# Banks, half tiles, placed turns and split casts in a fused linear-attention and gated-FFN kernel

## The chip, the core and the metric

The kernel runs on one core of one Trainium2 chip. A core has TensorE (PE, matrix products, which write to PSUM), VectorE (DVE), ScalarE (ACT), GpSimd (POOL) and SyncE (SP, here a queue that issues DMAs). Each engine works through its own queue in order and waits for the others by semaphores. PSUM is used here as one tile `ps` of 8 banks with 512 float32 columns each.

The metric is the device time of one execution in microseconds, as the median of several runs. The profile comes from one further execution and has its own time.

## The reference

Linear attention with a cosine weight, and behind it a feed-forward network with a GELU gate. B = 8 batches, H = 8 heads, S = 576 positions, D = 64; 4608 tokens, 512 channels, 1536 hidden columns:

```python
def phi(x, c, s):                       # c, s: cos and sin of pi/2 * pos/S
    r = np.maximum(x, 0.0)
    return np.concatenate([r * c, r * s], axis=-1)
q_p = phi(q, cos_w, sin_w)
k_p = phi(k, cos_w, sin_w)
kv = np.einsum('bhsf,bhsd->bhfd', k_p, v)
z = np.sum(k_p, axis=2)
num = np.einsum('bhsf,bhfd->bhsd', q_p, kv)
den = np.einsum('bhsf,bhf->bhs', q_p, z)[..., None] + 1e-06
attn = num / den
...
g = x @ w_gate                          # x: attn as [4608, 512]
gelu = 0.5 * g * (1.0 + erf(g * inv_sqrt2))
val = x @ w_val
out = gelu * val @ w_out
```

## The kernel before

**Tiles.** A batch of 576 positions is held as tiles j = 0 to 4. Tiles 0 to 3 have 128 rows; tile 4 has 64 positions, which stand in every other row of its 128, the rows between being zero. Tokens are split into blocks of the FFN: block 0 has 576 tokens (batch 0), the blocks after it 512 each, the last 448.

**Attention of a batch.** `scale` makes `qp` and `kp` (relu times cos, relu times sin) on DVE ("v") or ACT ("s"), `cast_v` the bfloat16 copy `vx` of v (line 138), four heads to an instruction. `kv_half(b, g)` makes kv and z of four heads with 20 matmuls (line 151), and `kv_evac` copies them out. `qp` is turned to `qT`: in batches 0 and 1 by PE (`q_by_pe`, line 311) and a copy out of PSUM (`q_evac`, line 317), later by a DMA (`turn_q`). `numer_mm(b, t, bank, g)` multiplies four heads of query tile t with kv (line 167); the two calls of a tile fill two banks. `norm` (lines 179 to 182) divides by the last column on DVE and writes `xb`; `numer` is both. `xb` is turned to channels by tokens, `xT`: in batches 0 and 1 by PE and a copy (`x_by_pe`, lines 325 to 329), later by a DMA (`turn_x`). Of tile 4 the copy takes every other column.

**FFN.** `gv_unit(n, jt, c0, w, gb, vb)` makes 128 hidden columns of w tokens: four matmuls g into bank gb (line 213), GELU on ACT (line 218), four matmuls v into bank vb (line 222), and the product to `hT` on DVE (line 226). `o_tile` multiplies 128 tokens of `hT` by the output weights in twelve matmuls (line 245), which `o_half` splits in two; `o_store` copies the sum on ACT (line 275) and issues the store.

**Order.** It is written out by hand: each engine runs its instructions in the order of the text. Batch 0 has nothing to run beside it, so its units of jt 0 to 3 are cut into pieces of tokens, and between them stand the numerators, turns and copies of the query tiles 1 to 4 (lines 371 to 414). `dummies` are matmuls of zeros that fill PE's time. Numerators of batch 0 all go to banks 6 and 7. POOL issues the weights in four steps: two of them before, two after x0 is written (lines 385 to 387), then the output weights, and when their first half has landed, SP loads q, k and v of batch 1 (lines 417 to 423). Then jt 4 to 11 run in pairs of 256 and 320 tokens. Lines 429 to 486 hold the last units of block 0, its output tiles with batch 1's attention between them, and batch 1's first units. From there on `run_block(n)` runs a block's 12 units, and the table `after` places the work of the next batch behind them: for n = 1 to 6 batch n + 1 is scaled, cast (line 516) and run through `attn_step`; each block also holds the output tiles of the one before.

Of the kernel before, what the change touches and what calls it, by code (L numbers as in the profile page):

```python
# [12 lines left out]
ALU = mybir.AluOpType  # L13
# [3 lines left out]
def kernel(  # L17
# [35 lines left out]
    ps = pp.tile([128, 8, 512], FP32, name="ps")  # L53
# [5 lines left out]
    xT = sb.tile([128, CT, N_TOK], BF16, name="xT")  # L59
# [5 lines left out]
    qT = [sb.tile([128, NJ + 1, H, 128], BF16, name=f"qT{i}") for i in range(2)]  # L65
# [4 lines left out]
    ident = sb.tile([128, 128], BF16, name="ident")  # L70
# [89 lines left out]
    def kv_evac(b, g, bank, eng):  # L160
        src = ps[:, bank, 0:4 * (D + 1)].rearrange("p (h e) -> p h e", e=D + 1)
        dst = kv[b % 2][:, 4 * g:4 * g + 4, 0:D + 1]
        (nc.scalar.copy if eng == "s" else nc.vector.tensor_copy)(dst, src)

    def numer_mm(b, t, bank, g):
        for h in range(4 * g, 4 * g + 4):
            nc.tensor.matmul(  # L167
                ps[:, bank + g, (h % 4) * (D + 1):(h % 4 + 1) * (D + 1)],
                lhsT=qT[b % 2][:, t, h, :],
                rhs=kv[b % 2][:, h, 0:D + 1],  # L170
                start=True, stop=True,
            )

    def norm(xb, bank, g0, g1):

        n = g1 - g0
        nd = ps[:, bank + g0:bank + g1, 0:4 * (D + 1)].rearrange("p g (h e) -> p g h e", e=D + 1)
        den = rot.tile([128, 2, 4], FP32, name="den")
        nc.vector.tensor_scalar(den[:, 0:n], nd[:, :, :, D], EPS, None, op0=ALU.add)
        rec = rot.tile([128, 2, 4], FP32, name="rec")  # L180
        nc.vector.reciprocal(rec[:, 0:n], den[:, 0:n])
        nc.vector.tensor_tensor(  # L182
            xb[:, g0:g1], nd[:, :, :, 0:D],
            rec[:, 0:n, :, None].to_broadcast([128, n, 4, D]), op=ALU.mult,
        )

    def new_xb():
        return rot.tile([128, 2, 4, D], BF16, name="xb", bufs=4)

    def numer(b, t, bank):  # L190

        numer_mm(b, t, bank, 0)
        numer_mm(b, t, bank, 1)
        xb = new_xb()
        norm(xb, bank, 0, 2)
        return xb

    def turn_x(b, t, xb):
# [10 lines left out]
    def gv_unit(n, jt, c0, w, gb, vb, mid=()):  # L209

        p0 = starts[n] + c0
        for ct in range(CT):
            nc.tensor.matmul(  # L213
                ps[:, gb, 0:w], lhsT=wg_sb[:, ct, jt * 128:(jt + 1) * 128],
                rhs=xT[:, ct, p0:p0 + w], start=(ct == 0), stop=(ct == CT - 1),
            )
        gel = rot.tile([128, 512], FP32, name="gel", bufs=3)
        nc.scalar.activation(gel[:, 0:w], ps[:, gb, 0:w], AF.Gelu)  # L218
        for f in mid:
            f()  # L220
        for ct in range(CT):
            nc.tensor.matmul(  # L222
                ps[:, vb, 0:w], lhsT=wv_sb[:, ct, jt * 128:(jt + 1) * 128],
                rhs=xT[:, ct, p0:p0 + w], start=(ct == 0), stop=(ct == CT - 1),
            )
        nc.vector.tensor_mul(hT[n % 2][:, jt, 64 + c0:64 + c0 + w], gel[:, 0:w], ps[:, vb, 0:w])  # L226
# [12 lines left out]
            return rows[p0 // 2:(p0 + n) // 2, j:j + 6:5]  # L239
        return rows[:, NJ]  # L240

    def o_half(n, m, bank, half):
        c0 = 128 * m - starts[n] + 64
        for jt in range(6 * half, 6 * half + 6):
            nc.tensor.matmul(  # L245
                ps[:, bank, :], lhsT=hT[n % 2][:, jt, c0:c0 + 128], rhs=wo_sb[:, jt, :],
                start=(jt == 0), stop=(jt == JT - 1),
            )
        if half == 1:
            o_store(m, bank)  # L250

    def o_tile(n, m, bank):

        o_half(n, m, bank, 0)
        o_half(n, m, bank, 1)

    def o_last(m, bank):

# [36 lines left out]
    def load_q(b):  # L295
        load(qf, q, b)
# [10 lines left out]
    def q_by_pe(b, j, bank, eng, h0=0, h1=H):  # L307

        qb = ps[:, bank, :].bitcast(BF16).rearrange("p (h t) -> p h t", h=H)
        for h in range(h0, h1):  # L310
            nc.tensor.transpose(out=qb[:, h, :], in_=qp[:, j, h, :], identity=ident)  # L311
        if eng is not None:
            q_evac(b, j, bank, eng, h0, h1)

    def q_evac(b, j, bank, eng, h0=0, h1=H):
        qb = ps[:, bank, :].bitcast(BF16).rearrange("p (h t) -> p h t", h=H)
        (nc.vector.tensor_copy if eng == "v" else nc.scalar.copy)(qT[b % 2][:, j, h0:h1], qb[:, h0:h1])  # L317

    def x_by_pe(b, t, xb, bank, eng, c0=0, c1=CT):
        p0 = b * S + t * 128  # L320
        cp = nc.vector.tensor_copy if eng == "v" else nc.scalar.copy
        xb2 = xb.rearrange("p g h d -> p (g h d)")
        view = ps[:, bank, 0:256].bitcast(BF16).rearrange("p (c t) -> p c t", c=CT)
        for ct in range(c0, c1):
            nc.tensor.transpose(out=view[:, ct], in_=xb2[:, ct * 128:(ct + 1) * 128], identity=ident)  # L325
        if t < NJ:
            cp(xT[:, c0:c1, p0:p0 + 128], view[:, c0:c1])  # L327
        else:
            cp(xT[:, c0:c1, p0:p0 + 64], view[:, c0:c1, 0:128:2])
# [8 lines left out]
    a4, b4 = (0, 4), (4, 8)  # L338
# [27 lines left out]
    q_evac(0, 0, 0, "v", *b4)  # L366
    q_evac(0, 1, 1, "v", *b4)
    kv_evac(0, 0, 4, "s")
    dummies(1, 7)
    kv_half(0, 1, 5, "s")  # L370
    x0 = new_xb()
    numer_mm(0, 0, 6, 0)
    norm(x0, 6, 0, 1)
    dummies(1, 4)
    numer_mm(0, 0, 6, 1)
    norm(x0, 6, 1, 2)
    q_evac(0, 2, 2, "s", *a4)
    dummies(1, 5)
    x_by_pe(0, 0, x0, 4, "s", 0, 2)
    dummies(2, 5)  # L380
    x_by_pe(0, 0, x0, 4, "s", 2, 4)
    x1 = numer(0, 1, 6)
    q_evac(0, 2, 2, "s", *b4)

    nc.gpsimd.tensor_copy(tiny[0:1, 1:2], x0[0:1, 1, 3, D - 1:D])
    load_w(4, 8)
# [1 line left out]


    A, Bw = (0, 256), (256, 320)  # L390
    gv_unit(0, 0, 0, 128, 0, 1)
    gv_unit(0, 1, 0, 128, 5, 4)
    x_by_pe(0, 1, x1, 0, "s")
    q_evac(0, 3, 3, "s", *a4)
    x2 = numer(0, 2, 6)
    gv_unit(0, 0, 128, 128, 5, 1)
    gv_unit(0, 1, 128, 128, 0, 4)
    q_evac(0, 3, 3, "s", *b4)
    x_by_pe(0, 2, x2, 2, "v")
    x3 = numer(0, 3, 6)  # L400
    gv_unit(0, 2, *A, 5, 1)
    q_by_pe(0, 4, 3, "s")
    gv_unit(0, 3, *A, 0, 4)
    x_by_pe(0, 3, x3, 2, "s")
    x4 = numer(0, 4, 6)
    gv_unit(0, 0, 256, 128, 5, 1)
    gv_unit(0, 1, 256, 128, 0, 4)
    gv_unit(0, 0, 384, 128, 5, 1)
    gv_unit(0, 1, 384, 128, 0, 4)
    x_by_pe(0, 4, x4, 3, "v")  # L410
    gv_unit(0, 2, *Bw, 5, 1)
# [84 lines left out]
    def L(f, *a):  # L496
        return lambda: f(*a)
# [78 lines left out]
```

## Time and profile before

| | |
|---|---|
| median of 3 runs | 334.9 us (334.8 to 335.13) |
| the profiled execution | 334.5 us, its span 332.4 us |
| TensorE clock granted, mean | 0.997 |
| four matmuls of 128, 256, 320, 512 columns, start to start | 0.22, 0.44, 0.54, 0.86 us |
| DVE product of 128x512 / of 128x128 | 0.69 / 0.29 us |
| GELU of 128x512 / of 128x128 on ACT | 0.60 / 0.28 us |
| cast of four heads of v (128x1280) on DVE / on ACT | 0.95 / 1.25 us |
| copy of 128x512 bfloat16 out of PSUM on DVE / on ACT | 0.41 / 0.59 us |

The span runs from the first to the last instruction; the time of the execution has 2.1 us around it. A row of the order of time has start, duration, engine, line, operation, output, inputs, shape and count, and in brackets the idle time of the engine before it and who ended it. Rows of several matmuls run into one another, since a matmul's duration includes its way through the array; where PE is free is read from the distance of starts.

### The profile page before, as it was taken

How to read it: one execution, taken by the hardware profiler on the slowest of the kernel's cores; microseconds unless marked ns; L12 is line 12 of the kernel's file. 1: busy time of each engine (PE TensorE's matmuls, PEld its weight loads, DVE VectorE, ACT ScalarE, POOL GpSimd, SP SyncE). 2: the span in 40 equal slices, each digit the busy share in tenths (PEclk: the TensorE clock that was granted, in tenths of full speed). 3: DMA queues.
4: the chain of work that ended last, by engine and by line, in shares of the span. 5: the costliest groups of instructions: out<-in, count | busy, mean ns of one | idle time of the engine just before them, and what ended most of it. 6: DMA issues, size and time to landing. Idle time of an engine off the chain costs nothing.

```text
span 332.4 us, 6000 instructions
## 1 busy us (share of the span) xinstructions
PE 322.4 (97%) x2281; PEld 171.3 (52%) x2281; DVE 177.2 (53%) x397; ACT 150.3 (45%) x278; POOL 19.7 (6%) x39
## 2 busy tenths in 40 slices
PE   7888999999999999999999999999999999999995
PEld 2576866755445444544455445444455444444443
DVE  5965478876674548454755576457635323222210
ACT  6764469683473237423742275226532322322321
POOL 2350010000100001000100010001000100000000
PEclk9999999999999999999999999999999999999998
DMA  7999988999379945996499449983723021000024
GB/s 237 257 186 207 240 299 268 318 219 351 66 123 247 345 80 100 263 333 95 86 263 321 110 77 210 374 132 59 180 48 77 20 65 32 32 34 32 34 65 95
DMA packets 84381, 54.66 MB, mean 164 GB/s; under 512 B 49408, under 2 KB 79872, under 8 KB 84352
## 3 DMA queue, kind: packets, MB, share of 16 engines
q1 hardware_dynamic: 78128, 49.10, 58.1%
q0 software_dynamic: 5792, 4.72, 9.4%
q10 hardware_dynamic: 432, 0.46, 0.4%
q8 instruction: 18, 0.29, 0.4%
q14 instruction: 11, 0.09, 0.1%
HBM read 37.75 MB, written 9.44 MB: 142 GB/s over the span
## 4 chain that ended last, share of the span: by engine, by line
PE 89%; DVE 5%; ACT 2%; issue 1%; DMA 1%; DVEq 0%; ACTq 0%
PE ps L245 27%; PE ps L213 26%; PE ps L222 26%; PE ps L167 3%; PE ps L124 3%; DVE vx L138 3%; PE ps L151 2%; PE ps L311 1%; PE ps L264 1%; ACT kp L134 1%; DMA out_dram<-o_sb 1%; DVE hT L226 1%; PE ps L325 1%; ACT gel L218 0%; DVE xb L182 0%
## 5 line engine op out<-in xcount | busy, mean ns | idle before, releaser
L226 DVE TENSOR_TENSOR hT<-gel,ps 128x512 bf16<-128x512 f32 (+5 forms) x130 | 77.0, 596 | 131.3 <-PE ps L222 128.1
L213 PE MATMUL ps<-xT,wg_sb 128*128 128x512 bf16 (+5 forms) x520 | 114.7, 343 | 1.4 <-ACT xT L327 0.7
L222 PE MATMUL ps<-xT,wv_sb 128*128 128x512 bf16 (+5 forms) x520 | 114.6, 343 | 0.8 <-DVE hT L226 0.8
L218 ACT ACTIVATE gel<-ps 128x512 f32<-128x512 f32 (+5 forms) x130 | 68.2, 525 | 84.7 <-PE ps L213 83.4
L245 PE MATMUL ps<-wo_sb,hT 128*128 128x512 bf16 x420 | 96.2, 379 | 0.0
L222 PEld LDWEIGHTS <-wv_sb 128*128 128x128 bf16 x520 | 49.1, 98 | 46.2 <-issue 1.0
L213 PEld LDWEIGHTS <-wg_sb 128*128 128x128 bf16 x520 | 47.0, 98 | 41.1 <-issue 1.5
L245 PEld LDWEIGHTS <-hT 128*128 128x128 bf16 x420 | 40.2, 98 | 45.9
L275 ACT COPY o_sb<-ps 128x512 f32<-128x512 f32 x35 | 20.5, 585 | 75.9 <-PE ps L245 72.8
L182 DVE TENSOR_TENSOR xb<-ps,rec 128x512 bf16<-128x512 f32 (+1 forms) x41 | 27.8, 679 | 1.5
L134 ACT ACTIVATE kp<-kf,sin_c 128x512 bf16<-128x512 f32 (+1 forms) x41 | 25.3, 679 | 0.5 <-DMA kf<-in_k_dram 0.5
L132 DVE TENSOR_SCALAR qp<-qf,cos_c 128x512 bf16<-128x512 f32 (+1 forms) x45 | 21.3, 516 | 0.7 <-DMA qf<-in_q_dram 0.7
L167 PEld LDWEIGHTS <-qT 128*128 128x128 bf16 x320 | 15.2, 98 | 9.2 <-issue 2.0
L134 ACT ACTIVATE qp<-qf,sin_c 128x512 bf16<-128x512 f32 (+1 forms) x31 | 19.2, 664 | 0.2 <-DMA qf<-in_q_dram 0.2
L132 DVE TENSOR_SCALAR kp<-kf,cos_c 128x512 bf16<-128x512 f32 (+1 forms) x45 | 18.0, 451 | 1.1 <-DMA kf<-in_k_dram 1.1
L167 PE MATMUL ps<-kv,qT 128*128 128x65 bf16 x320 | 17.0, 193 | 0.6 <-ACT qT L317 0.3
L206 POOL COPY xT<-xr 128x256 bf16<-128x256 bf16 x6 | 2.4, 400 | 205.3 <-DMA xr<-xb 205.3
L124 PE MATMUL ps<-junk 128*128 128x512 bf16 x37 | 11.4, 451 | 1.7 <-DVE par_i L101 1.7
L151 PEld LDWEIGHTS <-kp 128*128 128x128 bf16 x320 | 11.1, 97 | 3.5 <-issue 2.5
L151 PE MATMUL ps<-vx,kp 128*128 128x65 bf16 x320 | 11.9, 193 | 0.5
L138 DVE CAST vx<-vf 128x1280 bf16<-128x1280 f32 (+1 forms) x13 | 11.7, 934 | 0.3 <-DMA vf<-in_v_dram 0.3
L231 POOL COPY hT<-hT 128x768 bf16<-128x768 bf16 x8 | 7.6, 946 | 40.1 <-DVE hT L226 40.1
(54 smaller groups left out, 91.8 us busy)
## 6 DMA issues: line engine op xcount, KB each, us to landing
out_dram<-o_sb SPq DMA_DIRECT2D x38, 128.0 KB, 2.4
qf<-in_q_dram SPq DMA_DIRECT2D x7, 640.0 KB, 6.1
kf<-in_k_dram SPq DMA_DIRECT2D x7, 640.0 KB, 7.6
out_dram<-o_sb SPq DMA_DIRECT2D x16, 256.0 KB, 3.5
vf<-in_v_dram SPq DMA_DIRECT2D x6, 640.0 KB, 9.1
qf<-in_q_dram SPq DMA_DIRECT2D x7, 512.0 KB, 4.7
kf<-in_k_dram SPq DMA_DIRECT2D x7, 512.0 KB, 6.5
vf<-in_v_dram SPq DMA_DIRECT2D x6, 512.0 KB, 8.3
```

The source lines that it names most:

```text
L124: nc.tensor.matmul(ps[:, bank, :], lhsT=junk[:, 0:128], rhs=junk, start=True, stop=True)
L132: nc.vector.tensor_scalar(d, s, col, 0.0, op0=ALU.mult, op1=ALU.max)
L134: nc.scalar.activation(d, s, AF.Relu, scale=col)
L138: cp(vx[b % 2][:, :, h0:h1, 0:D], vf[:, h0:h1].rearrange("p h j d -> p j h d"))
L151: nc.tensor.matmul(ps[:, bank, (h % 4) * (D + 1):(h % 4 + 1) * (D + 1)], lhsT=kp[:, j, h, :], rhs=vx[b % 2][:, j, h, 0:D + 1], start=(j == ...
L167: nc.tensor.matmul(ps[:, bank + g, (h % 4) * (D + 1):(h % 4 + 1) * (D + 1)], lhsT=qT[b % 2][:, t, h, :], rhs=kv[b % 2][:, h, 0:D + 1], sta ...
L182: nc.vector.tensor_tensor(xb[:, g0:g1], nd[:, :, :, 0:D], rec[:, 0:n, :, None].to_broadcast([128, n, 4, D]), op=ALU.mult,)
L213: nc.tensor.matmul(ps[:, gb, 0:w], lhsT=wg_sb[:, ct, jt * 128:(jt + 1) * 128], rhs=xT[:, ct, p0:p0 + w], start=(ct == 0), stop=(ct == CT - 1),
L218: nc.scalar.activation(gel[:, 0:w], ps[:, gb, 0:w], AF.Gelu)
L222: nc.tensor.matmul(ps[:, vb, 0:w], lhsT=wv_sb[:, ct, jt * 128:(jt + 1) * 128], rhs=xT[:, ct, p0:p0 + w], start=(ct == 0), stop=(ct == CT - 1),
L226: nc.vector.tensor_mul(hT[n % 2][:, jt, 64 + c0:64 + c0 + w], gel[:, 0:w], ps[:, vb, 0:w])
L245: nc.tensor.matmul(ps[:, bank, :], lhsT=hT[n % 2][:, jt, c0:c0 + 128], rhs=wo_sb[:, jt, :], start=(jt == 0), stop=(jt == JT - 1),)
```

## The change

Four things change.

1. Batch 0: the numerators of tiles 1 to 4 get banks 0 and 1, those of tile 1 right behind those of tile 0; the q copies of tile 2 move ahead on ACT; one filler matmul goes. The turns (`X`) and the numerators (`Y`) of the tiles stand in other places among the pieces of units, some of them between g and v of a unit (the argument `mid`). The pieces use banks 4 to 7 (the last two 0 to 3).
2. The last query tile of batches 0 and 1: `q_evac` copies only its 64 used columns, so numerators, norm and turn run on 64 rows, and the copy to `xT` is without a step.
3. `o_half` becomes `o_part` with any range of hidden tiles; the fourth output tile of block 0 runs in four parts instead of two, the first of them between the two halves of the numerators of batch 1.
4. In every block from n = 2 to 6 the second half of v is cast by ACT; before, DVE cast both halves there.

```diff
-    def numer_mm(b, t, bank, g):
+    def numer_mm(b, t, bank, g, rows=128):
         for h in range(4 * g, 4 * g + 4):
             nc.tensor.matmul(
-                ps[:, bank + g, (h % 4) * (D + 1):(h % 4 + 1) * (D + 1)],
-                lhsT=qT[b % 2][:, t, h, :],
+                ps[0:rows, bank + g, (h % 4) * (D + 1):(h % 4 + 1) * (D + 1)],
+                lhsT=qT[b % 2][:, t, h, 0:rows],
                 rhs=kv[b % 2][:, h, 0:D + 1],
                 start=True, stop=True,
             )
...
-    def o_half(n, m, bank, half):
+    def o_part(n, m, bank, j0, j1):
         c0 = 128 * m - starts[n] + 64
-        for jt in range(6 * half, 6 * half + 6):
+        for jt in range(j0, j1):
...
-        if half == 1:
+        if j1 == JT:
             o_store(m, bank)
...
-        (nc.vector.tensor_copy if eng == "v" else nc.scalar.copy)(qT[b % 2][:, j, h0:h1], qb[:, h0:h1])
+        cp = nc.vector.tensor_copy if eng == "v" else nc.scalar.copy
+        if j < NJ:
+            cp(qT[b % 2][:, j, h0:h1], qb[:, h0:h1])
+        else:
+            cp(qT[b % 2][:, j, h0:h1, 0:64], qb[:, h0:h1, 0:128:2])
...
+        rows = 128 if t < NJ else 64
         view = ps[:, bank, 0:256].bitcast(BF16).rearrange("p (c t) -> p c t", c=CT)
         for ct in range(c0, c1):
-            nc.tensor.transpose(out=view[:, ct], in_=xb2[:, ct * 128:(ct + 1) * 128], identity=ident)
-        if t < NJ:
-            cp(xT[:, c0:c1, p0:p0 + 128], view[:, c0:c1])
-        else:
-            cp(xT[:, c0:c1, p0:p0 + 64], view[:, c0:c1, 0:128:2])
+            nc.tensor.transpose(
+                out=view[:, ct, 0:rows], in_=xb2[0:rows, ct * 128:(ct + 1) * 128], identity=ident[0:rows, 0:rows],
+            )
+        cp(xT[:, c0:c1, p0:p0 + rows], view[:, c0:c1, 0:rows])
...
     kv_evac(0, 0, 4, "s")
+    q_evac(0, 2, 2, "s", *a4)
     dummies(1, 7)
     kv_half(0, 1, 5, "s")
-    x0 = new_xb()
+    q_evac(0, 2, 2, "s", *b4)
+    x0, x1 = new_xb(), new_xb()
     numer_mm(0, 0, 6, 0)
     norm(x0, 6, 0, 1)
     dummies(1, 4)
     numer_mm(0, 0, 6, 1)
     norm(x0, 6, 1, 2)
-    q_evac(0, 2, 2, "s", *a4)
-    dummies(1, 5)
+    numer_mm(0, 1, 0, 0)
+    numer_mm(0, 1, 0, 1)
+    norm(x1, 0, 0, 2)
     x_by_pe(0, 0, x0, 4, "s", 0, 2)
     dummies(2, 5)
     x_by_pe(0, 0, x0, 4, "s", 2, 4)
-    x1 = numer(0, 1, 6)
-    q_evac(0, 2, 2, "s", *b4)
...
-    gv_unit(0, 0, 0, 128, 0, 1)
-    gv_unit(0, 1, 0, 128, 5, 4)
-    x_by_pe(0, 1, x1, 0, "s")
+    xs = {1: x1}
+
+    def X(t, bank, eng):
+        return lambda: x_by_pe(0, t, xs[t], bank, eng)
+
+    def Y(t):
+        def f():
+            xs[t] = numer(0, t, 0, 128 if t < NJ else 64)
+        return f
+
+    gv_unit(0, 0, 0, 128, 5, 6)
+    gv_unit(0, 1, 0, 128, 4, 7, (X(1, 2, "s"), Y(2)))
     q_evac(0, 3, 3, "s", *a4)
-    x2 = numer(0, 2, 6)
-    gv_unit(0, 0, 128, 128, 5, 1)
-    gv_unit(0, 1, 128, 128, 0, 4)
+    gv_unit(0, 0, 128, 128, 5, 6)
+    q_by_pe(0, 4, 2, None)
+    gv_unit(0, 1, 128, 128, 4, 7)
+    X(2, 5, "v")()
     q_evac(0, 3, 3, "s", *b4)
-    x_by_pe(0, 2, x2, 2, "v")
-    x3 = numer(0, 3, 6)
-    gv_unit(0, 2, *A, 5, 1)
-    q_by_pe(0, 4, 3, "s")
-    gv_unit(0, 3, *A, 0, 4)
-    x_by_pe(0, 3, x3, 2, "s")
-    x4 = numer(0, 4, 6)
-    gv_unit(0, 0, 256, 128, 5, 1)
-    gv_unit(0, 1, 256, 128, 0, 4)
-    gv_unit(0, 0, 384, 128, 5, 1)
-    gv_unit(0, 1, 384, 128, 0, 4)
-    x_by_pe(0, 4, x4, 3, "v")
-    gv_unit(0, 2, *Bw, 5, 1)
-    gv_unit(0, 3, *Bw, 0, 4)
-    gv_unit(0, 0, 512, 64, 5, 1)
-    gv_unit(0, 1, 512, 64, 0, 4)
+    q_evac(0, 4, 2, "s")
+    gv_unit(0, 2, *A, 4, 6, (Y(3),))
+    gv_unit(0, 3, *A, 5, 7)
+    X(3, 3, "s")()
+    Y(4)()
+    gv_unit(0, 0, 256, 128, 4, 6)
+    gv_unit(0, 1, 256, 128, 5, 7)
+    gv_unit(0, 0, 384, 128, 4, 6, (X(4, 2, "v"),))
+    gv_unit(0, 1, 384, 128, 5, 7)
+    gv_unit(0, 2, *Bw, 4, 6)
+    gv_unit(0, 3, *Bw, 5, 7)
+    gv_unit(0, 0, 512, 64, 0, 3)
+    gv_unit(0, 1, 512, 64, 1, 2)
...
     numer_mm(1, 1, 2, 0)
+    o_part(0, 3, 5, 0, 2)
     numer_mm(1, 0, 0, 1)
...
-    o_half(0, 3, 5, 0)
+    o_part(0, 3, 5, 2, 6)
     y2 = numer(1, 2, 6)
     x_by_pe(1, 0, y0, 0, "s")
-    o_half(0, 3, 5, 1)
+    o_part(0, 3, 5, 6, 9)
     x_by_pe(1, 1, y1, 1, "s")
+    o_part(0, 3, 5, 9, 12)
...
-    y4 = numer(1, 4, 2)
+    y4 = numer(1, 4, 2, 64)
...
-        put(4 + s, L(cast_v, b, 0, 4), L(cast_v, b, 4, 8, "s" if n == 1 else "v"))
+        put(4 + s, L(cast_v, b, 0, 4), L(cast_v, b, 4, 8, "s"))
```

`norm`, `numer` and the rest of `x_by_pe` get the same argument `rows` and work on `0:rows` of their tiles.

More of the change, by code (lines that the diff above doesn't have):

```diff
@@ L172, in numer_mm, with norm @@
             )
-    def norm(xb, bank, g0, g1):
+    def norm(xb, bank, g0, g1, rows=128):
         n = g1 - g0
-        nd = ps[:, bank + g0:bank + g1, 0:4 * (D + 1)].rearrange("p g (h e) -> p g h e", e=D + 1)
+        nd = ps[0:rows, bank + g0:bank + g1, 0:4 * (D + 1)].rearrange("p g (h e) -> p g h e", e=D + 1)
         den = rot.tile([128, 2, 4], FP32, name="den")
-        nc.vector.tensor_scalar(den[:, 0:n], nd[:, :, :, D], EPS, None, op0=ALU.add)
+        nc.vector.tensor_scalar(den[0:rows, 0:n], nd[:, :, :, D], EPS, None, op0=ALU.add)
         rec = rot.tile([128, 2, 4], FP32, name="rec")
-        nc.vector.reciprocal(rec[:, 0:n], den[:, 0:n])
+        nc.vector.reciprocal(rec[0:rows, 0:n], den[0:rows, 0:n])
         nc.vector.tensor_tensor(
-            xb[:, g0:g1], nd[:, :, :, 0:D],
-            rec[:, 0:n, :, None].to_broadcast([128, n, 4, D]), op=ALU.mult,
+            xb[0:rows, g0:g1], nd[:, :, :, 0:D],
+            rec[0:rows, 0:n, :, None].to_broadcast([rows, n, 4, D]), op=ALU.mult,
         )
@@ L188, in new_xb, with numer @@
         return rot.tile([128, 2, 4, D], BF16, name="xb", bufs=4)
-    def numer(b, t, bank):
-        numer_mm(b, t, bank, 0)
-        numer_mm(b, t, bank, 1)
+    def numer(b, t, bank, rows=128):
+        numer_mm(b, t, bank, 0, rows)
+        numer_mm(b, t, bank, 1, rows)
         xb = new_xb()
-        norm(xb, bank, 0, 2)
+        norm(xb, bank, 0, 2, rows)
         return xb
@@ L248, in o_half @@
             )
-        if half == 1:
+        if j1 == JT:
             o_store(m, bank)
     def o_tile(n, m, bank):
-        o_half(n, m, bank, 0)
-        o_half(n, m, bank, 1)
+        o_part(n, m, bank, 0, JT)
     def o_last(m, bank):
```

## The prediction

> **What bounds the kernel now.** I read the first page, then the list of waits of TensorE (PE), then PE's order of time in three stretches, then the same stretches on VectorE (DVE) and ScalarE (ACT), and last the DMA landings. The page:
>
> ```profile
> span 332.4 us, 6000 instructions
> PE 322.4 (97%) x2281; PEld 171.3 (52%) x2281; DVE 177.2 (53%) x397; ACT 150.3 (45%) x278; POOL 19.7 (6%) x39
> PE 89%; DVE 5%; ACT 2%; issue 1%; DMA 1%; DVEq 0%; ACTq 0%
> ```
>
> PE is busy for 322.4 of 332.4 us and 89% of the chain that ended last runs on it. So time can only come from the stalls of PE and from PE work that goes away. The busy time of a matmul includes its drain, so short stalls hide in it: I count a stall by the distance of starts. Four in a row of 128 columns start 0.22 us after each other (18.41 to 18.63), of 256 columns 0.435, of 320 columns 0.545, of 64 columns 0.12, eight numerator matmuls take 0.26 (60.54 to 60.80).
>
> PE in order of time, first batch (columns: start, duration, engine and line, what, count, idle before and who ended it):
>
> ```profile
> 20.16 0.38 PE L213 MATMUL ps<-xT,wg_sb 128*128 128x128 bf16 x4 [0.42 <-ACT xT L327]
> 21.84 0.30 PE L167 MATMUL ps<-kv,qT 128*128 128x65 bf16 x4 [0.27 <-ACT qT L317]
> 26.61 0.38 PE L222 MATMUL ps<-xT,wv_sb 128*128 128x128 bf16 x4 [0.49 <-DVE hT L226]
> 28.24 0.72 PE L213 MATMUL ps<-xT,wg_sb 128*128 128x320 bf16 x4 [0.58 <-DVE xT L329]
> 31.23 0.28 PE L222 MATMUL ps<-xT,wv_sb 128*128 128x64 bf16 x4 [0.30 <-DVE hT L226]
> 31.35 0.60 PE L213 MATMUL ps<-xT,wg_sb 128*128 128x256 bf16 x4
> ```
>
> Each wait names one step of the chain numerators, norm, turn, copy to xT, next unit. From 17.71 (first g of the FFN) to 31.35 (`gv_unit(0, 4)`) are 13.64 us. The work in it: sixteen 128-column groups of four 3.57, four of 256 1.74, four of 320 2.18, four of 64 0.48, four turns 0.89, three numerators 0.78, eight q transposes 0.445: 10.09 us. **3.55 us is stall**, and from 31.35 on PE runs gapless to 58.4.
>
> The v casts: first PE in a block where ACT casts half of v (n = 1) and one where DVE casts both (n = 2), then DVE before the latter.
>
> ```profile
> 73.30 1.37 PE L151 MATMUL ps<-vx,kp 128*128 128x65 bf16 x40
> 103.69 1.62 PE L151 MATMUL ps<-vx,kp 128*128 128x65 bf16 x40
> ```
>
> ```profile
> 102.69 1.81 DVE L138 CAST vx<-vf 128x1280 bf16<-128x1280 f32 x2
> 104.42 0.67 DVE L226 TENSOR_TENSOR hT<-gel,ps 128x512 bf16<-128x512 f32 x1
> ```
>
> The same 40 matmuls take 1.37 and 1.62 us. Of the two DVE casts (0.95 each) the first ends at 103.65 and PE starts at 103.69, 0.15 after it was free (102.68 + 0.864); its 20 matmuls of heads 0 to 3 need 0.6, so it wants the second cast at 104.29 and gets it at 104.50. The 1.62 stands in all five blocks n = 2 to 6.
>
> **The change, part by part.**
>
> *First batch, PE.* I follow the new order with the durations above; a copy is used about 0.04 us after its end, a matmul group of four is read 0.4 after its start (transposes 19.09, copy 19.53).
> Tile 1's numerators now go at 16.12, where a filler matmul of 0.215 stood, into their own banks 0 and 1 (q copies out of them end at 15.37), so they don't wait for tile 0's norm. DVE norms tile 1 right after tile 0 (0.64 idle before it at 17.91 vanishes): xb1 is ready at 18.39, not 19.03. Tile 0's turns and copies (PE 16.59 and 17.33, ACT to 18.02) and so the third g matmul at 18.07 stay.
> Unit (0,0) ends at 18.41, g of (0,1) at 18.63. Turn 1 follows at once (18.63 to 18.85), numerators 2 to 19.11, v to 19.33. ACT copies turn 1 from 19.07 to 19.65 and the units of columns 128 to 255 start at 19.70 (before: 20.16), after a stall of 0.37. With the q transposes of tile 4 inside (0.445, before at 22.85) they end at 21.03. Turn 2 21.03 to 21.25 (xb2 20.43). The g of jt 2 waits 0.05 for a gelu in its bank; numerators 3 sit in that unit at 21.74, and their second half waits for no one, since ACT's last tile-3 q copy ends at 21.75. The jt 3 unit ends at 23.31, turn 3 waits 0.07 for xb3 (numerators 22.0, plus 0.19 to den, 0.44 to the multiply, 0.69: 23.32), numerators 4 end at 23.86. Units of columns 256 end at 24.75. In the first of columns 384 PE meets turn 4 at 24.97, and xb4 is ready at 25.18 behind DVE's product of jt 3: **a stall of 0.27, the largest that the new order adds**; behind it in PE's queue stand that unit's v and everything later. v then waits 0.07 for a product held up on DVE by norm 4, and the 320-column units wait about 0.13 for the copy of turn 4. Their bank pairs 4/6 and 5/7 and the 64-column units' banks 0/3 and 1/2 remove the 0.30 at 31.23; a g of jt 4 in bank 0 waits some 0.14 for the 64-column gelu.
> Sum from 18.07: work 10.09 - 0.11 (two g matmuls done) - 0.10 (turn 4) = 9.88, stalls 0.37 + 0.05 + 0.07 + 0.27 + 0.07 + 0.13 + 0.14 = 1.10: `gv_unit(0, 4)` at about 29.0 against 31.35. **Gain 2.35 us.**
> ACT's moved q copies of tile 2 run in its waits at 15.05 to 15.57 and 15.84 (0.48 start to start), before kv's second copy is due and before tile 0's turn at 16.91. Without this cover the latter would be late by up to 0.5.
>
> *Does the gain arrive?* What comes from memory doesn't shift. POOL issues the weights after x0 is written (17.26, unmoved); they, then q, k and v of batch 1, keep their landings:
>
> ```profile
> 36.21 1.37 SPq L78 DMA_DIRECT2D qf<-in_q_dram  x2
> 37.62 2.06 SPq L78 DMA_DIRECT2D kf<-in_k_dram  x2
> 39.78 3.17 SPq L78 DMA_DIRECT2D vf<-in_v_dram  x4
> ```
>
> With landing times of 6.3, 8.5 and about 8 us: q at 43.3, k at 47.5, v near 50. ACT would start sq(0,1) at 42.7 and waits to 43.3: the gelu of (0,11) behind it is 0.6 late, and its product is wanted only by the twelfth matmul of the output tile that starts at 44.7 (47.03 - 2.35). ACT would start sk(0,1) at 45.9 and waits to 47.5, 1.6 us; behind it the output tiles' copies and four k scales stand, and ACT's idle 0.87 + 0.44 + 0.31 before 54.2 takes it up. The casts at 52.7 have their v. I cost the lot at 0; cover gone, up to 1.6 is lost here.
>
> *Half tiles.* ACT's q copy of tile 4 halves, 1.01 to a 512-element copy's 0.59; strided reads are the unknown, 0.59 to 1.01, and neither is waited for. The half turn costs PE 0.12 instead of 0.22 (row of 64-column matmuls), twice. Half-row norms run as many elements per row: 0. For the numerators' weights I weigh the Trainium skill, "TensorE: Matmul & The Clock Gate", section "What happens when you issue a matmul": a weight load's time goes with its columns. L167's load takes 98 ns for 128 columns, so 64 columns would save 49 ns times 16, 0.8 us, if loads set the pace. But the eight matmuls start 32 ns apart, a third of a load: 65 columns against 30 ns for 64 in the FFN. Streaming sets it; the trace wins, 0 (range 0 to 0.3).
>
> *Second batch, split output tile.*
>
> ```profile
> 58.99 0.42 PE L167 MATMUL ps<-kv,qT 128*128 128x65 bf16 x8 [0.17 <-DVE kv L163]
> 64.59 0.38 PE L222 MATMUL ps<-xT,wv_sb 128*128 128x128 bf16 x4
> ```
>
> Two output matmuls (0.43) fill PE's gap of 0.33 before 58.99, so the second numerators come 0.10 later. From 59.32 to 64.55 DVE is busy without a break (four norms of 1.03, two q scales, a product), and the v at 64.59 waits for that product. All that PE wins before it, about 0.5, ends in this wait, which moves by +0.10. Turn 4 gives 0.10 back behind it. **Sum 0**; bounds -0.4 and +0.2.
>
> *Casts.* ACT is idle for 1.13 us before 102.88; the cast of 1.25 starts after the gelu of unit 4 (101.65) and ends at 102.9, just when the next gelu is due. kv's second half finds its data: 0.25 saved; the 0.15 before the first half stays, as DVE's own cast is unmoved. Five blocks: **1.25 us**, bounds 0 and 2.0. A rule speaks against it: "ScalarE: Activation LUTs", "Rules for kernel authors", sends plain elementwise work to VectorE as up to three times faster. Here the rows say 1.25 against 0.95. Taken alone it adds 0.3 a block, 1.5 in all; in the trace the two engines run beside each other and n = 1, which does it so, has the short 1.37. I take the rows.
>
> **Sum.** 2.35 + 0 + 1.25 = 3.6. The profiled execution took 334.5 us (span 332.4 and 2.1 around it), so 330.9; the median of the runs, 334.9, lies 0.4 above it: **331.3 us**, span 328.8.
>
> **Rivals.** (a) *The start's gain is eaten by loads*: ACT and DVE catch up with q, k and v of batch 1, whose landings are fixed by the weight queue. For: the 1.6 us wait above, and 0.7 of idle for q at 56.04 already. Against: ACT's idle time after it, PE has banks to run on. Whole loss: 334.9 - 1.25 = 333.65; chance 0.08. (b) *The casts give nothing*, as ACT's ends on the edge (102.9) and the gelu slips: 334.9 - 2.35 = 332.55. Against: n = 1. Chance 0.08. (c) *Slower*: ACT's cast stands in its queue ahead of gelu 5 and both kv copies. If v landed late, all would wait, and numerators with them: kv's copies (104.49) have some 2 us before numerators at 106.88. From a cast start of about 103.7 each microsecond is lost five times; at 104.4 it costs 3.5 and outweighs the start, at 104.8 5.5, giving 337. Against: v is issued around 74 and lands within 10.3 us, 16 us early. Chance 0.03. (d) The forecast: 0.81.
>
> **Numbers.** What can be told from no change is about 0.2%, 0.67 us. Unknown stalls of the start are good for 0.7 each way (3.55 less all stalls would be 1.1 more), casts up to 0.75 more, loads up to 1.6 less: 329.8 to 333.0, which takes in (b). Faster: (a), (b) and (d) all are; less some doubt of both at once, 0.93; same 0.04; slower 0.03.
>
> **What would show it.** g of jt 4 with 256 columns at 29.0 (over 30 refutes the start); a wait of 0.2 to 0.3 before turn 4; the first output tile near 44.7; DVE still gapless to the second batch's first product, now 2.3 earlier; kv rows of 1.37 with casts of 1.25 on ACT; blocks n = 2 to 5 33.8 apart, not 34.04. Wrong if the k scales delay PE after 47 or gelu 5 comes after 103.2 relative to the old clock.

## The result, and the profile after

The changed kernel takes 331.72 us (median of 6 runs, 331.2 to 333.56) where the kernel before takes 334.88 (6 runs, 334.62 to 335.13): ratio 0.9913, 95% interval 0.989 to 0.9937. The forecast was 331.3, its range 329.8 to 333.0. A second measurement, with the experiments, gave 331.94 against 334.62: 0.9916 (0.9902 to 0.993). The runs of the changed kernel lie further apart than those of the kernel before.

The page of the changed kernel: span, busy times, and the shares of the chain of waits:

```profile
span 329.8 us, 5965 instructions
PE 319.8 (97%) x2245; PEld 170.7 (52%) x2280; DVE 173.3 (53%) x392; ACT 155.9 (47%) x283; POOL 19.7 (6%) x39
PE 92%; DVE 2%; DMA 2%; ACT 1%; issue 1%; POOL 0%; DVEq 0%; POOLq 0%; ACTq 0%
```

DVE's part of the chain fell from 5% to 2%: in the kernel before, 3% are its casts of v (line 138), which are no longer among the chain's main lines. DMA's 2% is the load of k at the start of the kernel (5.30 us in the chain), not a wait that the change made. DVE's busy time fell by 3.9 us and ACT's rose by 5.6, for the most part the five casts. PE's own busy time is not to be compared: 35 of its 2280 matmul records are missing here.

PE in order of time, first batch of the changed kernel:

```profile
18.73 0.27 PE L213 MATMUL ps<-xT,wg_sb 128*128 128x128 bf16 x2 [0.35 <-ACT xT L332]
...
20.34 0.38 PE L213 MATMUL ps<-xT,wg_sb 128*128 128x128 bf16 x4 [0.20 <-ACT xT L332]
...
26.10 0.29 PE L329 MATMUL ps<-ident,xb 64*128 64x64 bf16 x4
26.32 0.40 PE L222 MATMUL ps<-xT,wv_sb 128*128 128x128 bf16 x4
...
29.77 0.60 PE L213 MATMUL ps<-xT,wg_sb 128*128 128x256 bf16 x4
```

The five named stalls of 0.27 to 0.58 are gone but for one of 0.20 (the 0.35 at 18.73 is the wait for the copy of tile 0's turn, which the order before has too, inside its row at 17.71); from the third g matmul (18.73) to the units of jt 4 (29.77) PE needs 11.04 us, where it took 13.28 (18.07 to 31.35).

One kv of a later block, PE, then the two casts on DVE and ACT:

```profile
102.39 1.37 PE L151 MATMUL ps<-vx,kp 128*128 128x65 bf16 x40
```

```profile
101.38 0.95 DVE L138 CAST vx<-vf 128x1280 bf16<-128x1280 f32 x1
```

```profile
100.34 1.25 ACT L138 CAST vx<-vf 128x1280 bf16<-128x1280 f32 x1
101.57 0.60 ACT L218 ACTIVATE gel<-ps 128x512 f32<-128x512 f32 x1
```

ACT's cast ends just as the next gelu may start, and kv runs its 40 matmuls in 1.37 us, without the inner wait that made them 1.62 before.

A table by stage shows where the time came from. All are distances between starts of matmuls in the profiles' orders of time; "again" is a second profile of the changed kernel:

| us | before | changed | again |
|---|---|---|---|
| start to third g matmul | 18.07 | 18.73 | 18.12 |
| to the first unit of jt 4 | 13.28 | 11.04 | 11.04 |
| to kv of batch 1 | 25.68 | 25.68 | 25.68 |
| to the first unit of 512 columns | 10.81 | 11.09 | 11.91 |
| to kv of batch 7 | 172.00 | 170.95 | 170.96 |
| to the end of the last matmul | 88.49 | 88.24 | 88.23 |
| sum | 328.33 | 325.73 | 325.94 |

The start won 2.24, the casts 1.30; **the stage between kv of batch 1 and the 512-column units lost 0.28 in one profile and 1.10 in the other**, where the prediction had 0. The first row is not the change's: over all profiles of this study kv of batch 0 starts between 13.79 and 14.61, with the order of the kernel before (14.42 in one) as with the new one.

### The profile page after: what moved, and what is told of

It is laid out like the page before. It is cut to its first block, busy times and chain, and to the rows that moved or that the text cites. A ratio compares the mean times of both kernels' runs of the same rounds, so it can differ in the third digit from the quotient of the medians.

```text
span 329.8 us, 5965 instructions
## 1 busy us (share of the span) xinstructions
PE 319.8 (97%) x2245; PEld 170.7 (52%) x2280; DVE 173.3 (53%) x392; ACT 155.9 (47%) x283; POOL 19.7 (6%) x39
## 2 busy tenths in 40 slices
DMA packets 84381, 54.66 MB, mean 166 GB/s; under 512 B 49408, under 2 KB 79872, under 8 KB 84352
## 4 chain that ended last, share of the span: by engine, by line
PE 92%; DVE 2%; DMA 2%; ACT 1%; issue 1%; POOL 0%; DVEq 0%; POOLq 0%; ACTq 0%
PE ps L213 28%; PE ps L245 28%; PE ps L222 27%; PE ps L151 3%; PE ps L167 3%; DMA kf<-in_k_dram 2%; PE ps L310 1%; DVE qp L132 1%; PE ps L263 1%; ACT kp L134 1%; PE ps L329 1%; DVE kp L132 1%; ACT xT L332 0%; ACT gel L218 0%; DVE xb L182 0%
## 5 line engine op out<-in xcount | busy, mean ns | idle before, releaser
L213 PE MATMUL ps<-xT,wg_sb 128*128 128x512 bf16 (+5 forms) x506 | 113.1, 342 | 1.5 <-ACT xT L332 0.5
L222 PE MATMUL ps<-xT,wv_sb 128*128 128x512 bf16 (+5 forms) x508 | 113.0, 342 | 0.8 <-DVE hT L226 0.4
L182 DVE TENSOR_TENSOR xb<-ps,rec 128x512 bf16<-128x512 f32 (+2 forms) x41 | 27.8, 678 | 1.5
L167 PEld LDWEIGHTS <-qT 128*128 128x128 bf16 (+1 forms) x320 | 15.2, 98 | 9.0 <-issue 1.7
L167 PE MATMUL ps<-kv,qT 128*128 128x65 bf16 (+1 forms) x320 | 16.7, 194 | 0.1
L124 PE MATMUL ps<-junk 128*128 128x512 bf16 x34 | 10.7, 471 | 1.8 <-DVE par_i L101 1.7
L151 PE MATMUL ps<-vx,kp 128*128 128x65 bf16 x320 | 11.1, 193 | 0.1
L138 ACT CAST vx<-vf 128x1280 bf16<-128x1280 f32 (+1 forms) x9 | 10.7, 1194 | 0.2 <-DMA vf<-in_v_dram 0.2
```

Source lines behind the costliest of these rows:

```text
L151: nc.tensor.matmul(ps[:, bank, (h % 4) * (D + 1):(h % 4 + 1) * (D + 1)], lhsT=kp[:, j, h, :], rhs=vx[b % 2][:, j, h, 0:D + 1], start=(j == ...
L167: nc.tensor.matmul(ps[0:rows, bank + g, (h % 4) * (D + 1):(h % 4 + 1) * (D + 1)], lhsT=qT[b % 2][:, t, h, 0:rows], rhs=kv[b % 2][:, h, 0:D ...
L182: nc.vector.tensor_tensor(xb[0:rows, g0:g1], nd[:, :, :, 0:D], rec[0:rows, 0:n, :, None].to_broadcast([rows, n, 4, D]), op=ALU.mult,)
L213: nc.tensor.matmul(ps[:, gb, 0:w], lhsT=wg_sb[:, ct, jt * 128:(jt + 1) * 128], rhs=xT[:, ct, p0:p0 + w], start=(ct == 0), stop=(ct == CT - 1),
L222: nc.tensor.matmul(ps[:, vb, 0:w], lhsT=wv_sb[:, ct, jt * 128:(jt + 1) * 128], rhs=xT[:, ct, p0:p0 + w], start=(ct == 0), stop=(ct == CT - 1),
```

## The experiments

The theory after the result: the start and the casts are worth what was predicted; what is missing comes from the half tiles (**S**: PE loses about 0.09 us at each change of the weight tile's shape). The rivals are the prediction's own sum for half tiles (P), and its rival (a), loads that keep their clock.

**e1, full tiles again.**

```diff
-        if j < NJ:
-            cp(qT[b % 2][:, j, h0:h1], qb[:, h0:h1])
-        else:
-            cp(qT[b % 2][:, j, h0:h1, 0:64], qb[:, h0:h1, 0:128:2])
+        cp(qT[b % 2][:, j, h0:h1], qb[:, h0:h1])
...
-    y4 = numer(1, 4, 2, 64)
+    y4 = numer(1, 4, 2)
```

> The changed kernel with its last query tile of batches 0 and 1 on all 128 rows again (q copy, numerators, norm, turn, copy). Theory S (PE loses about 0.09 us each time the shape of the weight tile changes): the two half numerators cost 0.19 each, the two half turns 0.19 less the 0.10 that their shorter stream saves, less about 0.1 hidden behind the wait for xb of tile 4 in batch 0; so this is faster than the changed kernel by about 0.45: 331.3 us. In its profile the eight numerator matmuls of tile 4 take 0.26 start to start and not 0.37, and the stretch from the v that waits for DVE in batch 1 to the first unit of 512 columns takes 3.25 us and not 3.45. Rival P (the prediction's sum: half turns save 0.10 each, half numerators cost nothing): slower by 0.2, 331.9. Rival N (no difference): 331.7.

331.21 us (330.89 to 331.97), ratio 0.9898 (0.9883 to 0.9913): on the side of S, though the intervals of the two kernels overlap. The profile decides. PE of the changed kernel in batch 1:

```profile
63.31 0.39 PE L329 MATMUL ps<-ident,xb 128*128 128x128 bf16 x4
63.63 0.44 PE L167 MATMUL ps<-kv,qT 128*64 128x65 bf16 x8
64.01 0.40 PE L213 MATMUL ps<-xT,wg_sb 128*128 128x128 bf16 x4
...
64.90 0.60 PE L222 MATMUL ps<-xT,wv_sb 128*128 128x256 bf16 x4
65.43 0.29 PE L329 MATMUL ps<-ident,xb 64*128 64x64 bf16 x4
65.65 0.61 PE L213 MATMUL ps<-xT,wg_sb 128*128 128x256 bf16 x4
```

and of e1:

```profile
62.79 0.39 PE L325 MATMUL ps<-ident,xb 128*128 128x128 bf16 x4
63.01 0.42 PE L167 MATMUL ps<-kv,qT 128*128 128x65 bf16 x8
63.27 0.39 PE L213 MATMUL ps<-xT,wg_sb 128*128 128x128 bf16 x4
...
64.28 0.60 PE L222 MATMUL ps<-xT,wv_sb 128*128 128x256 bf16 x4
64.72 0.39 PE L325 MATMUL ps<-ident,xb 128*128 128x128 bf16 x4
64.94 0.60 PE L213 MATMUL ps<-xT,wg_sb 128*128 128x256 bf16 x4
```

The pair of numbers before the shape of the output names the weight tile: 128*128, 128*64 or 64*128. From the start of the turn before them to the half numerators 0.32 pass instead of 0.22, from their own start to the next group 0.38 instead of 0.26; the half turn takes the same 0.22 as a whole one, and the v before it 0.53 instead of 0.44. So every entry into and every exit out of the other shape costs about 0.1, and the 0.10 that a half turn saves in streaming goes on its exit. The profile names no engine that is waited for there. It does show one thing that differs: the weight load. In e1 the first load for the numerators starts at 62.96, 0.05 before their first matmul; in the changed kernel it starts with it, at 63.63, and so at the other three changes of shape (64.00, 65.43, 65.65). A load takes about 0.1 (98 ns for 128*128, 110 for 128*64). The Trainium skill, "TensorEngine Tiling (Array Packing)", section "Key Properties", has a rule that may stand behind these rows: changing the array's tiling mode drains the engine. It states no time, nor that a weight tile of 64 rows or columns is such a change; if it is, these rows give its price here. Another rule could be meant: "TensorE: Matmul & The Clock Gate", section "Weight-path perf modes — Fast Weight Load (FWL) and DoubleRow", grants the fast weight load only to weights of 128 columns. But the half turn's weight has 64 rows and 128 columns, and pays as much.

From the v that waits for DVE to the 512-column units e1 takes 3.24 (62.57 to 65.81) and the changed kernel 3.45, as S said. But e1's whole stage from kv of batch 1 takes 11.15, no less than 11.09: something else took 0.26. It stands in front of the numerators of batch 1 in e1:

```profile
56.28 0.41 PE L167 MATMUL ps<-kv,qT 128*128 128x65 bf16 x8 [0.26 <-ACT kv L163]
```

**e2, casts alone** (the kernel before and the one edited line of the table `after`).

> The kernel before with the second half of v cast by ACT in blocks 2 to 6 and nothing else. Theory: the wait inside kv's 40 matmuls goes, 0.26 in each of five blocks: 334.88 - 1.3 = 333.6 us, kv rows of 1.37 us. Rival (b) of the prediction (ACT's cast delays the next gelu and nothing is gained): 334.9. Rival (the gain is twice as large, the wait before kv goes as well): 332.9.

333.18 us (332.82 to 333.77), ratio 0.9954 (0.9941 to 0.9967). The interval reaches from 1.1 to 2.0 us below 335.0, which holds the theory's 1.3 and, at its edge, the second rival's 2.0. The profile decides: the span shrank from 332.4 to 331.1, 1.3; kv's rows are 1.37 and blocks 33.78 us apart, where the kernel before has 34.04. So the inner wait of 0.26 went, and the one of 0.15 before kv stayed (103.57 to 103.72).

**e3, the start alone** (casts, full tiles and halves of the output tile as before).

> The changed kernel's new banks and order of the first batch alone: casts as before, tile 4 on 128 rows, the fourth output tile in two halves as before. Theory: the changed kernel won 2.24 us between the third g matmul (18.73 and 18.07) and the unit of jt 4 (29.77 and 31.35), of which half tiles had taken back some 0.2; all of it arrives, as the loads of batch 1 only use up idle time of ACT: 334.88 - 2.4 = 332.5 us. Rival (a) of the prediction (loads of batch 1 have a fixed clock and eat it): 334 or more. The gain counted from the third g matmul to jt 4 should be 2.3 to 2.5, and the first kv matmul of batch 1 should come earlier by the same amount.

332.54 us (331.86 to 333.12), ratio 0.9924 (0.991 to 0.9937). The start wins 2.31 (third g matmul 18.52, jt 4 29.49) and 25.68 follow up to kv. Then PE waits:

```profile
57.42 0.67 PE L167 MATMUL ps<-kv,qT 128*128 128x65 bf16 x16 [0.88 <-ACT kv L163]
```

and ACT shows why:

```profile
55.29 1.33 ACT L134 ACTIVATE qp<-qf,sin_c 128x512 bf16<-128x512 f32 x2 [0.66 <-DMA qf<-in_q_dram]
56.53 0.56 ACT L274 COPY o_sb<-ps 128x512 f32<-128x512 f32 x1
56.99 0.38 ACT L163 CAST kv<-ps 128x260 bf16<-128x260 f32 x1
```

Two q scales of **batch 2** wait for memory, and kv's copy stands behind them in ACT's queue. So rival (a) happens in part, by a wait that the prediction names (0.7 for q at 56.04) but judges for DVE alone. A chain leads to it: q of batch 1 lands late against the earlier PE, its scales end later, the load of q of batch 2 overwrites their source and is issued later. I call this **theory L**. The times bear it out: in all nine profiles in which ACT waits for q of batch 1, the load of q of batch 2 is issued 4.26 to 4.28 us after that wait ends (here 44.70 and 48.98).

**e6, more half numerators** (the last tile of batches 2 to 7 as well, with norms on 64 rows and the unused rows of `xb` set to zero by POOL).

```diff
-                lhsT=qT[b % 2][:, t, h, 0:rows],
+                lhsT=qT[b % 2][:, t, h, 0:128:2] if rows < 128 and b > 1 else qT[b % 2][:, t, h, 0:rows],
...
-            turn_x(b, i - 1, numer(b, i - 1, 6))
+            turn_x(b, i - 1, numer(b, i - 1, 6, 128 if i - 1 < NJ else 64))
```

> The changed kernel with the numerators of the last query tile on 64 rows in batches 2 to 7 as well (every other column of qT as weights, 64-row norm, the unused rows of xb set to zero by POOL). Six more half numerators. Theory S: two shape changes each, 6 x 0.19 = 1.1 us more: 332.8 us. Rival W (a weight load's time goes with its columns and sets the pace: 8 loads x 49 ns less in each): 2.3 us less, 329.4. Rival N: 331.7.

333.23 us (332.37 to 333.63), ratio 0.9949 (0.9932 to 0.9965): 1.5 above the changed kernel's first median, 1.1 to 1.2 by the ratios, where 1.1 was expected. Blocks are 34.00 us apart (kv at 102.04 and 136.04) where the changed kernel has 33.78 (102.39 and 136.17): 0.22 for each half numerator, two changes of shape. In batch 2 the numerators start 0.96 after the v before them instead of 0.87, and the next g 0.37 after that instead of 0.25; their first weight load starts with them (82.50), where it starts 0.22 ahead in the changed kernel (82.77 and 82.99). Rival W, that fewer weight columns speed it up, is out.

**Four runs beside each other: the changed kernel again, and three attempts.** e10, with full tiles as e1, moves one load, from behind the output weights to behind the input weights:

```diff
-    nc.gpsimd.tensor_copy(qf[0:2, 0, 0, 0:1], wo_sb[0:2, 5, C - 1:C])
+    nc.gpsimd.tensor_copy(qf[0:2, 0, 0, 0:1], wv_sb[0:2, CT - 1, J - 1:J])
     load_q(1)
+    nc.gpsimd.tensor_copy(kf[0:2, 0, 0, 0:1], wo_sb[0:2, 5, C - 1:C])
     load_k(1)
```

e7 has full tiles and `put((4 if n == 1 else 3) + s, ...)` for the casts, which places them one unit earlier. e8 has the edits of e10 and e7, and `sq(3, 0, "v"), sq(4, 0, "v")`, with the turn and the load behind them, moved behind `gv_unit(1, 1, 0, 128, 1, 5)`.

> The changed kernel once more, beside the runs below. Expected 331.7 us as measured, with a scatter of over 1 us where the kernel before has 0.5 to 1.0. Theory L (the start of the changed kernel runs so early that ACT's q scales of batch 2 wait for memory before kv's copies, by an amount that changes from one execution to the next): in this profile, if the q loads of batch 1 are issued by 36.3, the first numerators of batch 1 start within 1.5 us of kv's first matmul; where they are issued later than 36.8 after an early start, PE waits up to 0.9 there.

> The changed kernel with full tiles (as e1) and the loads of q of batch 1 issued when the last FFN input weights have landed (about 32) instead of after the first half of the output weights (about 36); k and v as before. Theory L: q is there when ACT and DVE come to it, so q of batch 2 is issued by PE's clock and PE's wait before the numerators of batch 1 (0.26 in e1, 0.88 in e3) goes: 330.9 us, and less scatter. Rival C (contention): the output weights land later by the 1.1 MB that go ahead, some 3 us, k and v too, and ACT's k scales delay what follows: 331.5 or more. Rival N (the wait was of no weight): 331.2.

> The changed kernel with full tiles (as e1), and in blocks 2 to 6 both casts of v placed one unit earlier, where DVE has 2.4 us without work before the product of unit 4. Theory: kv's wait of 0.15 for DVE's own cast goes in five blocks: 331.2 - 0.75 = 330.5 us; blocks 33.63 us apart instead of 33.78. Rival (ACT's scales and cast in one unit delay a gelu and PE with it): 331.2 or slower.

> The three together: full tiles, casts one unit earlier, q of batch 1 loaded earlier, and two q scales on DVE (with their turn and the next q load) moved behind the first two products of batch 1. Theory: DVE's unbroken run of work before the first product of batch 1 is 0.87 shorter, and the v that waits 0.41 for it starts at once: 331.2 - 0.26 - 0.75 - 0.4 = 329.8 us. If the split of the output tile is what DVE's chain swallowed, its stretch from the first kv matmul to the first unit of 512 columns shrinks to below 10.6 us, against 10.8 in the kernel before and 11.1 in the changed one. Rival (DVE's products come late behind the scales instead): no less than 330.2.

The changed kernel again: 331.94 (331.91 to 332.03), so its wide scatter did not come back. Its start was on time (kv of batch 0 at 13.91), the loads of q of batch 1 were issued at 36.69, and PE waited:

```profile
57.03 0.42 PE L167 MATMUL ps<-kv,qT 128*128 128x65 bf16 x8 [0.82 <-ACT kv L163]
57.28 0.59 PE L245 MATMUL ps<-wo_sb,hT 128*128 128x512 bf16 x2
57.71 0.42 PE L167 MATMUL ps<-kv,qT 128*128 128x65 bf16 x8
```

and on ACT:

```profile
54.89 1.33 ACT L134 ACTIVATE qp<-qf,sin_c 128x512 bf16<-128x512 f32 x2 [0.71 <-DMA qf<-in_q_dram]
```

In the first profile the whole start was 0.6 later and this wait was 0. So **an early start is paid back here**: kv of batch 1 began at 54.84 and 55.45, the numerators at 57.03 and 56.82. PE's wait, beside the issue of both q loads, in the profiles whose loads and scales stand where the changed kernel has them (e2 and e5 are as before, without a wait):

| | q of batch 1 | q of batch 2 | kv of batch 1 | PE waits |
|---|---|---|---|---|
| before | 36.21 | 49.61 | 57.03 | 0 |
| changed | 36.83 | 48.26 | 55.45 | 0 |
| e6 | 35.64 | 47.44 | 54.86 | 0 |
| e1 | 36.10 | 47.94 | 54.66 | 0.26 |
| e4 (below) | 36.87 | 48.31 | 54.82 | 0.39 |
| again | 36.69 | 47.87 | 54.84 | 0.82 |
| e3 | 37.31 | 48.98 | 55.17 | 0.88 |
| e7 | 37.55 | 49.15 | 54.68 | 1.57 |

Where the second load leads kv by 7.19 us or more PE doesn't wait; below it does, the more the less lead there is. One row (again, lead 6.97) waits more than its lead says: ACT had q of batch 2 only 7.02 after its issue there, and 6.13 to 6.33 after it in e1, e3, e4 and e7.

e10: 331.71 (331.35 to 332.55), ratio 0.9912 (0.9897 to 0.9927), 0.5 above e1 where 0.3 below was expected. A miss: q was issued at 32.78 and ACT still waited for it until 44.55 (in e1, issued at 36.10, until 43.67), and PE for kv's copy for 0.69.

```profile
44.55 0.72 ACT L134 ACTIVATE qp<-qf,sin_c 128x512 bf16<-128x512 f32 x1 [1.35 <-DMA qf<-in_q_dram]
```

The output weights, issued at about 21, were still in transfer: their second half landed 21.4 us after its issue, where e1 has 18.5. So the loads delayed each other, which rival C had named, and issuing this one earlier gained nothing.

e7: 331.22 (330.77 to 331.68), 0.9894 (0.9879 to 0.9909). Blocks are 33.62 apart, as expected, 0.16 less in each of five, yet its time is e1's where 0.7 less was expected: its profile has the largest wait of all, 1.57, from loads issued at 37.55. The profiled run was the slowest of its four (331.68); whether the others had less of the wait, one profile can't say.

e8: 330.85 (330.32 to 331.24), 0.9878 (0.9862 to 0.9894). The v that waits for DVE's product, in the changed kernel and in e8:

```profile
62.30 0.39 PE L213 MATMUL ps<-xT,wg_sb 128*128 128x128 bf16 x4
63.09 0.38 PE L222 MATMUL ps<-xT,wv_sb 128*128 128x128 bf16 x4 [0.41 <-DVE hT L226]
```

```profile
62.95 0.39 PE L213 MATMUL ps<-xT,wg_sb 128*128 128x128 bf16 x4
63.41 0.38 PE L222 MATMUL ps<-xT,wv_sb 128*128 128x128 bf16 x4
```

A g of this size needs 0.22 to the next start; 0.79 passed and now 0.46. So 0.33 of this wait went with the two scales that left DVE's run of work, and 0.24 remain (DVE's product starts at 63.08 and takes 0.29). The wait for q (0.85) remains too. Better than the changed kernel, short of the 329.8.

**e11, the scales behind.** If the load can't come earlier, what waits for it can stand elsewhere (with e7's full tiles and earlier casts):

```diff
-    sq(0, 0, "v"), sq(0, 1, "s")
-    sq(1, 0, "v"), sq(1, 1, "s")
-    sq(2, 0, "v")
     o_tile(0, 2, 4)
...
-    sq(2, 1, "s"), sq(3, 1, "s"), sq(4, 1, "s")
-    turn_q(2, 0, 3)
+    sq(0, 0, "v")
+    for j in range(NJ + 1):
+        sq(j, 1, "s")
```

with the rest of DVE's scales, and the turns and loads behind them, after the first products of batch 1.

> The changed kernel with full tiles and casts one unit earlier (as e7), and the q scales of batch 2 no longer ahead of kv's copies: on ACT all five behind kv's first copy, on DVE one behind the second copy, two behind the first two products of batch 1, two behind turn 4, each turn of q and the next q load behind its scales. e10 and e8 showed that q issued at 32.8 still lands at 44.5, as the weights fill the DMA engines, so the wait must be moved and not the load. Theory L: PE no longer waits for ACT's kv copy (0.82 in after_again, 1.57 in e7) and no longer 0.41 for DVE's product; from kv's first matmul to the first unit of 512 columns 10.6 us or less, in any execution: 331.2 - 1.2 = 330.0 us. Rival Q (the turns of q by DMA now come some 5 to 10 us later and the numerators of batch 2 wait for them): 331 or more, with PE idle before numerators after the kv of batch 2.

330.89 us (330.42 to 331.44), ratio 0.9886 (0.9873 to 0.9899). PE in the disputed stage and in block 2:

```profile
54.69 1.37 PE L151 MATMUL ps<-vx,kp 128*128 128x65 bf16 x40
55.92 0.41 PE L167 MATMUL ps<-kv,qT 128*128 128x65 bf16 x8
...
65.25 1.03 PE L213 MATMUL ps<-xT,wg_sb 128*128 128x512 bf16 x3
...
86.05 1.02 PE L213 MATMUL ps<-xT,wg_sb 128*128 128x512 bf16 x4 [0.47 <-issue]
```

The wait for kv is gone, and the stage takes 10.56. The fair rows beside it are e1 and again, whose q of batch 2 was issued as here (47.94 and 47.87; here 47.88) and whose PE waited 0.26 and 0.82; e7's loads were later by more than 1 us. So the last link of theory L, scales ahead of kv's copy in ACT's queue, is confirmed by taking it away. But 0.5 comes back at 86.05, where block 2 begins. It reads x of batch 2, which SP turns by DMA; the four turns took SP 8.33 us here and 7.20 in e7, with q, k and v loads just ahead of them. The profile names no engine for this wait, and what delayed the start was not separated; rival Q named the q turns, and their numerators (from 73.64 on) did not wait. The span is 328.4, the least of all; the median equals e8's and misses the 330.0 that was expected.

**e5, half tiles alone, and e4, no split.**

> The kernel before with the half tiles alone (last query tile of batches 0 and 1 on 64 rows), order, banks, output tile and casts as before. Theory S (0.09 us of PE at each change of the weight tile's shape): two numerators and two turns, 2 x 0.19 + 2 x (0.19 - 0.10) = 0.56 us at most, some of it inside waits that batch 0 had anyway: 0.2 to 0.5 slower than the kernel before, 334.9 to 335.1 if that is at 334.7; the eight numerator matmuls of tile 4 in batch 1 followed by the next g 0.37 after they start, not 0.26. Rival P (prediction): 0.2 faster, from half turns.

> The changed kernel with the fourth output tile in two halves, as before. Prediction: the split is worth nothing, since DVE's unbroken run of norms and scales up to batch 1's first product sets the time: within 0.2 of the changed kernel, 331.8. From the second kv copy on DVE to that product the same 5.8 us with and without the split. Rival (the split wins the 0.33 of PE's gap or the 0.24 before the second g): 332.2.

e5: 334.7 (13 runs, 334.22 to 334.82) against 334.77, ratio 0.9993 (0.9984 to 1.0001). Neither S's loss nor P's gain. The profile has both: from jt 4 to the 512-column units it takes 36.69 instead of 36.49, the 0.2 of S; but from the third g matmul to jt 4 12.93 instead of 13.28, as two shorter copies come just where the old order waits: ACT's of q tile 4 (0.59 instead of 1.01), which lets the v behind DVE's product wait 0.24 instead of 0.49, and DVE's of turn 4 (0.28 instead of 0.42). In the new order these waits are gone or covered, and e1 is not slower there (10.98, changed 11.04).

e4: 331.72 (331.21 to 334.65), ratio 0.9927 (0.9901 to 0.9954): no difference from the changed kernel that these runs can tell. From DVE's kv copy to its first product pass 5.80 us in e4 (56.29 to 62.09) and 5.84 in the changed kernel (56.92 to 62.76). But the two profiles differ in one thing: in e4 PE waited for ACT's kv copy.

```profile
56.57 0.67 PE L167 MATMUL ps<-kv,qT 128*128 128x65 bf16 x16 [0.39 <-ACT kv L163]
```

The wait cost nothing there, since the second numerators could follow at once, 2.01 after kv's first matmul (56.57 and the 0.26 that eight take; 1.96 before the change). With the split, two output matmuls stand between them, and every wait is paid in full: the second numerators start 2.05 after kv without a wait, 2.31 in e1 (wait 0.26), 2.87 in again (0.82), 3.62 in e7 (1.57). DVE's stretch of 5.8 becomes 6.28 in again and 6.27 in e7, and stays 5.84 in e3, which has no split and a wait of 0.88. So in the profiles **the split costs about 0.4 where kv's copy is late**, and nothing where it is not; the medians don't resolve it.

## Why the prediction was right

- **First batch, 2.35:** right, 2.24 (and 2.30 with full tiles; the prediction's own terms sum to 29.05, a gain of 2.30). The stall before turn 4, put at 0.27, was 0.21; the copy of turn 1 let PE wait 0.36 between starts where 0.37 was put; the g of jt 4 at 29.0 holds in e1 (28.98).
- **Loads cost 0:** the step that failed. The waits for q and k of batch 1 came, smaller than put (0.42 and 0.28 on ACT, for 0.6 and 1.6), and were taken up: 25.67 to 25.69 up to kv in every profile. But the q of batch 2 depends on those scales, and ACT has kv's copy behind it. The prediction gives the 0.7 of idle as a point for rival (a), and does not follow it to what stands behind. Cost: 0 to 0.82 in the changed kernel, some 0.4 of it by the split output tile.
- **Half tiles, 0 for numerators, 0.10 saved per turn:** wrong in sign. Load time against streaming was the wrong pair to weigh; the price is the change of shape, about 0.1 each way. In batch 1 it took 0.2 where 0.1 was to come. Nor does the page's rule, less time for fewer columns, come out of these traces: a load of 64 columns took 110 ns and one of 128 columns 98.
- **Split output tile, 0:** right where kv's copy is on time. PE won some 0.5 and lost it at the v behind DVE's unbroken run, where PE loses 0.57 between starts now (0.79 less 0.22). e8 and e11 take DVE's work out of that run, and 0.24 of it remain. Where kv's copy is late the split costs about 0.4, by the second numerators behind it; the prediction had no late copy.
- **Casts, 1.25:** right, 1.30; ACT's cast ended where it was put. The rule on plain work for VectorE would have had this slower; on a path that another engine's idle time shortens, it is the wrong question.
- **Sum:** 2.24 + 1.30 - 0.28 = 3.26 in the first profile, less 0.66 of a late start that is not the change's; 2.24 + 1.30 - 1.10 = 2.44 in the second. The medians fell by 3.2 and 2.7. The forecast was 3.6. Some of its nearness is luck: the span missed by more (329.8 and 330.0, for 328.8), but the 0.4 that the prediction adds for the step from profile to median did not come (331.86 profiled, median 331.72).

What stays open: how often, and how long, an execution of the changed kernel waits for q; only profiled ones show it.

## What to carry to other kernels

When a stage gets faster, list what comes from memory behind it, and follow each load to the next one that waits for its buffer, and each instruction that waits for it to what stands behind it in the same queue. Work put into a gap to fill it delays what follows by its whole length once the gap has moved. A tile with half its rows unused was not cheaper on PE here, where it changed the weight tile's shape for a few matmuls; use the half for copies and leave the matmuls whole. An instruction moved to an engine that is slower at it can still win, if that engine is idle then and the first engine's second instruction was the one waited for.

## What the runs showed of the hardware that was not expected

A change of PE's weight tile between 128*128 and 128*64 or 64*128 costs about 0.1 us each way, where the profile names no engine as waited for (0.22 for a pair in six more places, e6); the first weight load behind the change starts with its matmul, and up to 0.22 ahead of it where the shape stays. Loads of q issued 3.3 us earlier than in e1 landed 0.9 later (44.55 and 43.67), beside weights still in transfer. And the start of the kernel moves by up to 0.8 us between profiles. In the changed kernel's first one, 0.74 later than the kernel before, DVE got the second half of k 0.25 later (7.65 and 7.40), and a scale of q took 0.60 instead of 0.33 (at 12.42); POOL was issuing weights then, but so it was in the kernel before. Why some executions have it wasn't tried.
